# Moving one unit's scan by a slot or two, splitting three weight additions, and reordering loads in a scan-plus-MLP kernel

## The chip, the cores and the metric

The kernel runs on one core of one Trainium2 chip. The time is the device time of one execution in microseconds (us). The span that a profile covers is the part from the first to the last recorded instruction; the time is 1.7 us longer than its span. Before the change the median of the first three runs was 353.07 us (352.94 to 353.20).

## The reference

Two blocks follow each other. The first is a state-space scan (batch 4, 8 heads, 768 positions, head size 32, state size 16). The second multiplies its output, 3072 rows of 256, by a 256 x 2048 matrix, applies SiLU and multiplies by a 2048 x 256 matrix. All is in fp32.

```python
# first block, per chunk of the sequence (a clipped to [1e-6, 1])
L = exp(cum[i] - cum[j]) * (i >= j)            # decay between positions
y = ((C @ B.T) * L) @ x + (C @ state) * exp(cum)
state = decay_full * state + sum_j B_j x_j decay_from_j
# second block
h = x @ w_in
out = (h / (1 + exp(-h))) @ w_out
```

## The kernel before

The 3072 rows are cut into 12 units of 256 rows. Each unit goes through a scan: loads, transposes of its B and C (here `bn`, `tbc`), a decay matrix E by a VectorE scan over `ab`, B times decay (`BT`, on GpSimd), state products, and a product `y`, copied to `XM` by ScalarE. XM then feeds the first matrix product (`f_s1`, eight slots a unit, four matmuls each) and the second (`f_s2`). The scan's steps of later units are strewn between the slots of earlier ones, by hand, so that TensorE always has a matmul ready.

The loads of one unit stand on one queue in this order:

```python
def load_unit(u):
    load_pa(u, nc.sync)
    ...
    load_ab(u, nc.sync)        # clamped and scanned by VectorE
    load_n(u, 0, nc.sync)      # bn: transposed by TensorE
    load_x(u, nc.sync)
```

The weights come as raw pieces of 128 x 2 x 256 pairs of 32-bit words and are rebuilt on chip: two ScalarE activations (`w_size`), three VectorE operations, then one addition on GpSimd (`w_bits`, cut here):

```python
def w_bits(n, parts=1):
    ...
    for i in range(parts):
        fs = slice(WF // parts * i, WF // parts * (i + 1))
        nc.gpsimd.tensor_tensor(out=dst[:, :, fs]..., in0=u[:, :, fs], in1=v[:, :, fs], op=ALU.add)
```

A slot of the first product; `hp` comes from a pool of three PSUM buffers:

```python
def f_s1(g, j):
    hp = ps_h.tile([128, 2, UT], FP32, name="hp")
    for i in range(2):
        f = 2 * j + i
        for kc in range(KC):
            nc.tensor.matmul(out=hp[:, i], lhsT=w_in_sb[:, kc, f*128:(f+1)*128], rhs=xm[:, kc], ...)
    nc.scalar.activation(GTS[g][:, :, j], hp, AF.Silu)
```

The places of unit 2's steps (E = decay scan, D = BT, T and C = transposes and what follows, G = state products and masks, Y = y and XM; b and s = weight pieces), as (unit, slot, what follows the slot):

```python
steps = ((1, 0, "b5 s6"), (1, 1, "b6 s7"), (1, 2, "b7 s8"), (1, 3, "b8"), (0, 4, "E D"),
         (1, 4, ""), (0, 5, "T C s9"), (1, 5, "b9 s10"), (0, 6, "G"), (1, 6, "b10 s11"),
         (0, 7, "Y b11 s12"), (1, 7, "b12 s13"))
```

The loop over unit 3's slots, with unit 5's steps in between:

```python
for j in range(8):
    f_s1(3, j)
    ...
    scan_piece(5, j, ("", "", "T", "E", "DCS", "G", "YS", ""))
    ...
    f_s2(2 if j in (5, 6) else 4)
```

The very end of the kernel writes two last output tiles: each is transposed by TensorE, copied out of PSUM (one by ScalarE, one by VectorE) and stored, one from the SyncE queue and one from the ScalarE queue.

## Time and profile before

| | before |
|---|---|
| median of 3 runs | 353.07 us |
| the execution that was profiled | 355.06 us, span 353.3 us |
| TensorE busy | 343.8 us, 97% |
| TensorE weight loads | 287.5 us, 81% |
| VectorE, ScalarE, GpSimd busy | 58%, 46%, 32% |
| idle gaps of TensorE from 15 us to the last outputs | 3.05 us in six places |

The six gaps are read from the timeline of TensorE, where a bracket behind a group of instructions gives the idle time before it and what ended it. Those lines are in the prediction.

### The profile page before, as it was taken

To read this page: it belongs to the slowest core of one execution; us is meant where nothing else is said; L and a number is where in the kernel's file an instruction comes from. 1 tells how busy PE (TensorE), PEld (TensorE's weight loads), DVE (VectorE), ACT (ScalarE), POOL (GpSimd) and SP (SyncE) were. 2 spreads that over 40 slices of the span, in tenths; PEclk is the share of its full clock that TensorE was granted. 3 is DMA by queue.
4 is the path that set the end of the run, shared out by engine and by line. 5 is a ranking of instruction groups with operands and counts; after the bars stand their busy time and mean duration, and the time that the engine had idled before them with its cause. 6 is when DMAs were issued, how large, how long until landed. Compare 5 with 4: busy or idle time off the path is not lost.

```text
span 353.3 us, 8349 instructions
## 1 busy us (share of the span) xinstructions
PE 343.8 (97%) x3308; PEld 287.5 (81%) x3308; DVE 204.4 (58%) x408; ACT 162.0 (46%) x394; POOL 111.5 (32%) x137
## 2 busy tenths in 40 slices
PE   8979999999999999999999999999999999999995
PEld 3658778888888888888888888888888888888883
DVE  6997879978586663553664563564652232234821
ACT  2567487233323645454645445544545454453100
POOL 4344335554085041244041244041234112051200
PEclk9999999999999999999999999999999999999999
DMA  6986895699649398958179956057404237522202
GB/s 107 225 243 161 174 371 108 125 194 210 132 99 154 81 185 164 184 104 147 32 146 185 172 98 105 16 98 143 92 2 74 51 61 142 90 46 38 36 4 46
DMA packets 117376, 42.79 MB, mean 121 GB/s; under 512 B 102488, under 2 KB 109144, under 8 KB 117336
## 3 DMA queue, kind: packets, MB, share of 16 engines
q1 hardware_dynamic: 110328, 25.67, 34.7%
q0 software_dynamic: 4464, 16.25, 24.9%
q10 hardware_dynamic: 2544, 0.33, 0.6%
q8 instruction: 26, 0.43, 0.6%
q14 instruction: 14, 0.11, 0.1%
HBM read 22.83 MB, written 3.15 MB: 74 GB/s over the span
## 4 chain that ended last, share of the span: by engine, by line
PE 75%; DVE 9%; DMA 8%; SPq 5%; issue 2%; ACT 0%; ACTq 0%; DVEq 0%
PE o_ps L627 32%; PE hp L682 28%; PE hp L491 4%; PE hp L627 3%; DMA out_dram<-ot 2%; DMA ab<-in_a_dram 2%; SPq L95 2%; PE o_ps L613 2%; PE gy L467 2%; DVE E L303 1%; DVE E L415 1%; DMA raw<-in_moe_w_out_dram 1%; SPq L107 1%; PE gy L458 1%; DMA gT<-in_a_dram 1%
## 5 line engine op out<-in xcount | busy, mean ns | idle before, releaser
L685 DVE TENSOR_TENSOR gT<-hp,p 128x256 f32<-128x256 f32 x64 | 26.9, 420 | 73.8 <-ACT p L696 37.9
L491 PE MATMUL hp<-XM,w_in_sb 128*128 128x256 f32 x256 | 59.6, 382 | 2.0 <-POOL w_in_sb L182 2.0
L627 PE MATMUL o_ps<-gT,w_out_sb 128*128 128x256 f32 x240 | 60.4, 379 | 0.0
L688 ACT ACTIVATE gT<-gT 128x256 f32<-128x256 f32 x96 | 39.7, 414 | 44.0 <-DVE gT L685 43.9
L491 PEld LDWEIGHTS hp<-XM,w_in_sb 128*128 128x128 f32 x256 | 47.9, 190 | 10.0 <-POOL w_in_sb L182 3.3
L682 PE MATMUL hp<-raw 128*128 128x256 f32 x192 | 52.7, 380 | 0.0
L544 POOL TENSOR_TENSOR ps<-ps 128x256 f32<-128x256 f32 x35 | 29.2, 835 | 72.3 <-ACT ps L574 71.0
L627 PEld LDWEIGHTS o_ps<-gT,w_out_sb 128*128 128x128 f32 x240 | 45.4, 190 | 6.3
L539 POOL DMA_DIRECT2D gT<-gT x31 | 27.4, 921 | 64.9 <-PE hp L682 22.3
L682 PEld LDWEIGHTS hp<-raw 128*128 128x128 f32 x192 | 36.2, 190 | 5.4 <-POOL ps L544 0.6
L696 ACT ACTIVATE p<-hp 128x256 f32<-128x256 f32 x64 | 24.5, 383 | 27.5 <-PE hp L682 26.1
L685 DVE TENSOR_TENSOR gT<-hp,u 128x256 f32<-128x256 f32 x32 | 13.6, 425 | 39.3 <-PE hp L682 39.3
L682 PE MATMUL hp<-XM,w_in_sb 128*128 128x256 f32 x128 | 34.1, 389 | 0.0
L493 ACT ACTIVATE gT<-hp 128x512 f32<-128x512 f32 x32 | 19.0, 594 | 28.3 <-PE hp L491 28.2
L682 PEld LDWEIGHTS hp<-XM,w_in_sb 128*128 128x128 f32 x128 | 23.3, 190 | 4.3 <-issue 1.0
L303 DVE TENSOR_TENSOR_SCAN E<-ab,diag 128x256 f32<-128x256 f32 (+1 forms) x32 | 25.6, 842 | 0.4
L574 ACT ACTIVATE ps<-o_ps 128x256 f32<-128x256 f32 x38 | 14.4, 382 | 23.9 <-PE o_ps L627 22.2
L340 POOL TENSOR_TENSOR BT<-bn,E 128x256 f32<-128x256 f32 x12 | 9.0, 748 | 50.2 <-DVE E L303 48.9
L627 PE MATMUL o_ps<-gT,wu 128*128 128x256 f32 x88 | 22.4, 380 | 0.0
L627 PE MATMUL o_ps<-gT,wv 128*128 128x256 f32 x88 | 22.2, 380 | 0.0
L627 PE MATMUL o_ps<-gT,raw 128*128 128x256 f32 x80 | 20.6, 382 | 0.0
L682 PE MATMUL hp<-raw,w_in_sb 128*128 128x256 f32 x64 | 19.1, 380 | 0.0
(125 smaller groups left out, 518.7 us busy)
## 6 DMA issues: line engine op xcount, KB each, us to landing
gT<-gT POOLq DMA_DIRECT2D x31, 512.0 KB, 6.0
ab<-in_a_dram SPq DMA_DIRECT2D x40, 128.0 KB, 3.9
raw<-in_moe_w_in_dram SPq DMA_DIRECT2D x8, 512.0 KB, 6.3
raw<-in_moe_w_out_dram SPq DMA_DIRECT2D x8, 512.0 KB, 6.5
xt<-in_x_dram SPq DMA_DIRECT2D x24, 128.0 KB, 5.7
out_dram<-ot SPq DMA_DIRECT2D x92, 32.0 KB, 2.5
bn<-in_B_dram SPq DMA_DIRECT2D x22, 64.0 KB, 4.8
tbc<-in_C_dram SPq DMA_DIRECT2D x40, 32.0 KB, 1.8
```

The lines of the kernel that those rows point to most:

```text
L303: nc.vector.tensor_tensor_scan(out=E[u].rearrange("p k h t -> p (k h t)")[:, Q * g0:Q * (g0 + n)], data0=t.rearrange("p g t -> p (g t)"), ...
L340: engine.tensor_tensor(out=BT[u], in0=bn[u], in1=E[u][:, :, :, Q - 1:Q].to_broadcast([128, 2, H, N]), op=ALU.mult)
L491: nc.tensor.matmul(out=hp[:, i], lhsT=w_in_sb[:, kc, f * 128:(f + 1) * 128], rhs=xm[:, kc], start=(kc == 0), stop=(kc == KC - 1))
L493: nc.scalar.activation(GTS[g][:, :, j], hp, AF.Silu)
L539: nc.gpsimd.dma_start(out=o[:, js], in_=a[:, js], accum_op=ALU.add)
L544: engine.tensor_tensor(out=o, in0=p, in1=q, op=op)
L574: nc.scalar.activation(pn, on, AF.Copy)
L627: nc.tensor.matmul(out=o, lhsT=w(j), rhs=g()[:, j], start=(j == 0), stop=(j == last))
L682: nc.tensor.matmul(out=o, lhsT=w, rhs=x_, start=start, stop=True, skip_group_check=True)
L685: nc.vector.tensor_tensor(out=o, in0=p, in1=q, op=ALU.add)
L688: nc.scalar.activation(o, i, AF.Silu)
L696: nc.scalar.activation(o, i, AF.Copy)
```

## The change

The intent is to take away each of the six waits. Weight pieces 1 to 3 are added in halves, so that TensorE can begin on the first half. Unit 2's scan takes its transposes a slot earlier and its other steps one to two slots later. `bn` is loaded ahead of `ab`. Unit 2's y comes ahead of the first matmuls of the second product, and unit 5's y comes behind two of them.

```diff
 def load_unit(u):
+        load_n(u, 0, nc.sync)
         load_ab(u, nc.sync)
-        load_n(u, 0, nc.sync)
         load_x(u, nc.sync)
...
 def f_X(u):
-        nc.scalar.activation(XM[u], DP.pop(u)[:, :, 0:128], AF.Copy)
+        y = DP.pop(u)
+        n = 2 if u < 2 else 4
+        for i in range(0, 4, n):
+            nc.scalar.activation(XM[u][:, i:i + n], y[:, i:i + n, 0:128], AF.Copy)
...
-    w_bits(1)
+    w_bits(1, 2)            # and the same for pieces 2 and 3
...
-    steps = (..., (1, 3, "b8"), (0, 4, "E D"), (1, 4, ""), (0, 5, "T C s9"), (1, 5, "b9 s10"),
-             (0, 6, "G"), (1, 6, "b10 s11"), (0, 7, "Y b11 s12"), (1, 7, "b12 s13"))
+    steps = (..., (1, 3, "b8"), (0, 4, ""), (1, 4, "T"), (0, 5, "E D s9"), (1, 5, "C b9 s10"),
+             (0, 6, ""), (1, 6, "G b10 s11"), (0, 7, "b11 s12"), (1, 7, "Y b12 s13"))
...
 for j in range(8):           # unit 2's slots
+        f_s2(4 if j == 0 else 0)
         f_s1(2, j)
-        f_s2(2)
+        f_s2(2 if j > 0 else 0)
         ...
-        if j > 1:
-            f_s2(2)
+        f_s2(2 if j > 2 else 0)
...
 for j in range(8):           # unit 3's slots
         f_s1(3, j)
+        if j == 6:
+            f_s2(2)
         ...
-        f_s2(2 if j in (5, 6) else 4)
+        f_s2((4, 4, 4, 4, 4, 2, 0, 4)[j])
```

The rest of the diff makes a small helper tile (`mark`) five words smaller.

More of the change, by code (lines that the diff above doesn't have):

```diff
@@ L205 @@
     load_x(1, nc.sync)
-    mark = const.tile([1, RAW], U32, name="mark")
+    mark = const.tile([1, RAW - 5], U32, name="mark")
     for n in range(3, RAW):
         if n > 4:
-            nc.sync.dma_start(out=mark[:, n:n + 1], in_=raw[n - 2][0:1, 0, 0, 0:1])
+            nc.sync.dma_start(out=mark[:, n - 5:n - 4], in_=raw[n - 2][0:1, 0, 0, 0:1])
         load_w(n, nc.sync)
@@ L828 @@
     f_B(1)
-    w_bits(2)
+    w_bits(2, 2)
     f_C(1)
@@ L839 @@
     w_size(4)
-    w_bits(3)
+    w_bits(3, 2)
     w_bits(4)
@@ L845 @@
     f_s1(0, 3)
-    steps = ((1, 0, "b5 s6"), (1, 1, "b6 s7"), (1, 2, "b7 s8"), (1, 3, "b8"), (0, 4, "E D"),
-             (1, 4, ""), (0, 5, "T C s9"), (1, 5, "b9 s10"), (0, 6, "G"), (1, 6, "b10 s11"),
-             (0, 7, "Y b11 s12"), (1, 7, "b12 s13"))
+    steps = ((1, 0, "b5 s6"), (1, 1, "b6 s7"), (1, 2, "b7 s8"), (1, 3, "b8"), (0, 4, ""),
+             (1, 4, "T"), (0, 5, "E D s9"), (1, 5, "C b9 s10"), (0, 6, ""), (1, 6, "G b10 s11"),
+             (0, 7, "b11 s12"), (1, 7, "Y b12 s13"))
     def w_steps(todo):
```

## The prediction

> **What bounds the kernel now.** I read the page first, then the waits of TensorE, then the timeline of TensorE, then what each waited-for engine was doing at that time.
>
> ```profile
> PE 343.8 (97%) x3308; PEld 287.5 (81%) x3308; DVE 204.4 (58%) x408; ACT 162.0 (46%) x394; POOL 111.5 (32%) x137
> PE   8979999999999999999999999999999999999995
> ```
>
> TensorE is busy 97% of the span, and only the first three slices and the last fall short of nine tenths. A plain step of the products is one matmul, shown as two records; the timeline shows eight records (four matmuls) each 1.73 us, or 0.216 us a record. I call four such matmuls of the first product a slot. This change alters no matmul's shape or number, so it can win only idle time. All of it after 15 us stands in the timeline of TensorE, as the lines with a bracket:
>
> ```profile
> 18.14 1.99 PE L491 MATMUL hp<-XM,w_in_sb 128*128 128x256 f32 x8 [0.34 <-POOL w_in_sb L182]
> 22.07 1.99 PE L491 MATMUL hp<-XM,w_in_sb 128*128 128x256 f32 x8 [0.94 <-POOL w_in_sb L182]
> 26.21 14.08 PE L491 MATMUL hp<-XM,w_in_sb 128*128 128x256 f32 x64 [0.73 <-POOL w_in_sb L182]
> 40.59 0.75 PE L355 MATMUL o_ps<-ident,bn 128*128 128x128 f32 x2 [0.30 <-DMA bn<-in_B_dram]
> 50.15 0.69 PE L458 MATMUL gy<-cw,sm 32*64 32x64 f32 x32 [0.50 <-DVE E L415]
> 107.96 0.69 PE L458 MATMUL gy<-cw,sm 32*64 32x64 f32 x32 [0.24 <-DVE E L415]
> ```
>
> The columns are start, duration and instruction; the bracket is the idle time before it and who ended it. The sum is 0.34 + 0.94 + 0.73 + 0.30 + 0.50 + 0.24 = 3.05 us, 0.9% of the span. The transposes at 40.59 also take 0.75 us where the two just after them (tbc) take 0.38, because the second half of bn lands later: 0.37 us more, 3.42 in all. These six places are the targets: pieces 1 to 3 of the weights, the transposes of unit 2's bn, and the y of units 2 and 5. From 110 us to the end there is no wait, so what is won by then stays won and nothing more can be.
>
> **What the Trainium skill says.** "Perfetto Trace Analysis", section "Identifying the Most-Contended Engine", says that busy matmul time is no measure of nearness to the limit; so I took the gaps, and the equal 0.216 us steps between them, rather than the 97%. "GPSIMD Engine Reference", section "3.1 Elementwise", gives each GpSimd instruction a fixed dispatch cost, so halves should cost more in sum than a whole. The trace agrees: piece 0, already halved, takes 1.72 us, a whole piece 1.27. "SBUF — State Buffer", section "Who interferes with whom", has VectorE and GpSimd exclude each other from a shared pair of ports in some operations. The trace agrees: the shift on L176 takes 0.43 us alone and 1.37 beside a GpSimd addition (35.79). "DMA: Bandwidth & Descriptors", section "Queues, rings and completion order", has each DMA engine take a ring's descriptors in order; so what bn gains by going ahead of ab, ab loses. No run has shown this yet.
>
> **Part 1: pieces 1 to 3 in halves.**
>
> ```profile
> 14.46 1.72 POOL L182 TENSOR_TENSOR w_in_sb<-wu,wv 128x256 uint32<-128x256 uint32 x2 [3.06 <-DVE wv L178]
> 16.81 1.27 POOL L182 TENSOR_TENSOR w_in_sb<-wu,wv 128x512 uint32<-128x512 uint32 x1 [0.63 <-DVE wv L178]
> ...
> 20.76 1.26 POOL L182 TENSOR_TENSOR w_in_sb<-wu,wv 128x512 uint32<-128x512 uint32 x1 [0.96 <-DVE wv L178]
> 24.89 1.27 POOL L182 TENSOR_TENSOR w_in_sb<-wu,wv 128x512 uint32<-128x512 uint32 x1 [2.87 <-DVE wv L178]
> ```
>
> The slot's first two matmuls read only the first half, ready after 1.72 / 2 = 0.86 us instead of 1.27: 0.41 us sooner. The second half is ready 0.86 us later, just when two matmuls (0.86) are through. The three gains do not add up. Each addition starts when VectorE has finished its piece (the bracket), and VectorE is busy from 11.7 to 24.8 us without waiting for TensorE; so each gain only uses up the same lead, and what remains after piece 3 is 0.41. The longer additions fall beside scans and reads of PSUM, so I count no loss on VectorE. XM of units 0 and 1 in two halves costs ScalarE some 0.16 us each (0.38 x 2 less 0.60), off the path. Gain so far: 0.41.
>
> **Part 2: bn before ab, and the transposes one slot earlier.** The queue issues ab from 30.52 to 36.45 and bn to 37.74 us. In the new order bn is issued by about 35.5 and should land about 37.3. TensorE reaches the transposes at 40.13 - 1.73 - 0.41 = 37.99. The wait should vanish: 0.30 + 0.37 = 0.67. Gain at the state products of unit 2: 1.08.
>
> Ab lands up to a microsecond later. Unit 2's E waits for it (VectorE starts at 40.45) and GpSimd ends BT at 44.60. With the scan's products one slot later TensorE asks for BT at 44.94 + 1.73 - 1.08 = 45.59, so the delay fits.
>
> **Part 3: y of unit 2.** Here I expect part of the gain to be lost. The hp tile has three buffers, so the seventh slot of unit 0 needs the activation of the slot three before, which stands on ScalarE behind a weight piece that waits for its load:
>
> ```profile
> 45.79 0.67 ACT L164 ACTIVATE wu<-raw 128x512 f32<-128x512 f32 x1 [3.02 <-DMA raw<-in_moe_w_out_dram]
> 46.36 0.67 ACT L166 ACTIVATE wv<-raw 128x512 f32<-128x512 uint32 x1
> 46.94 0.57 ACT L493 ACTIVATE gT<-hp 128x512 f32<-128x512 f32 x1
> ```
>
> It ends at 47.51. Before, that slot started at 47.65, so the wait did not show. Now TensorE is there at 45.59 + 0.98 (the state products) = 46.57 and waits about 1 us if the load lands as before: the gain falls to 0.1. Then y no longer waits, because both slots stand ahead of it (47.55 + 3.46 = 51.0, against E ready at 50.0): + 0.50. Four matmuls of the second product (1.73) cover the copy to XM, which on ScalarE may end at 54.1, just in time. So 0.6 if the load of that weight piece is unmoved, up to 1.6 if it comes a microsecond sooner. That can be: the queue now stands still at xt until 39.98 with bn's many small packets outstanding, and these now go out earlier. I choose 0.9.
>
> **Part 4: unit 5.** Bn goes ahead of ab for every unit, and unit 5 is the one with no slack:
>
> ```profile
> 98.20 1.06 DVE L321 TENSOR_SCALAR ab<-ab 128x1024 f32<-128x1024 f32 x1 [0.81 <-DMA ab<-in_a_dram]
> 99.34 0.07 DVE L322 MEMSET ab<- 128x16 f32 x1
> 99.52 3.01 DVE L303 TENSOR_TENSOR_SCAN E<-ab,diag 128x512 f32<-128x512 f32 x2
> ```
>
> Its two bn issues take 1.2 us of the queue, so ab lands some 1.2 us later. Against that, the scan is slowed now (3.01, against 2.34 for unit 2) by four GpSimd additions from 96.75 to 101.44; started later it falls clear of them: -0.39 on L321 and -0.67 on the scan. E should be about where it was, BT too (it ends at 103.61), while TensorE asks for it 0.9 sooner, at 103.0; so up to 0.6 of the gain turns into a new wait there. I take 0.3. Putting two matmuls (0.86) before y covers the 0.24 wait and any such lateness of E. XM of unit 5 is not used before 114 us. Net: -0.3 + 0.24.
>
> **Sum.** 0.9 - 0.3 + 0.24 = 0.84; I add 0.3 because the loads follow VectorE, which also moves forward if the weight piece lands sooner. About 1.1 us: 353.07 - 1.1 = 351.9.
>
> **Rivals.** First, all waits vanish and nothing takes their place. The sum is then 0.41 + 0.67 + 0.50 + 0.24 = 1.8, with the unmovable part of the weight waits left: 351.2. For it: each part is aimed at one bracket. Against it: the activation at 47.51, which was not visible as a wait because it was met by 0.14 us. Second, ab's later landing becomes the bound in unit 5: if the scan is not quicker, BT is 1.2 us later (104.8), and TensorE starts there at 104.8 instead of 103.89. That eats everything: 353.07 - 0.24 + 0.9, with y then free, about 353.7. Against it: the GpSimd additions that now lie beside the scan. Third, the second product catches up with its weights (pieces 10 to 15 on GpSimd from 51.48 on, one each 2.36 us); before, the first use of piece 10 came 7 us after it was ready (60.30 against 52.87), so I give this little.
>
> **Range and chances.** 351.9 us, 351.0 to 352.9. The total idle time bounds the gain at 1%, and the worst rival loses less than 0.3%, so within 2% is nearly certain: faster 0.01, same 0.98, slower 0.01.
>
> **What would show it.** In the changed trace: the three weight brackets smaller by about 0.4 in total; no bracket on bn's transposes; a new bracket of up to 1 us on the first product near 46.6, ended by ScalarE; none on y of unit 2; a small one on unit 5's state products, ended by GpSimd's BT. If that last one is over 1 us, or the first product's bracket is missing, the working is wrong there.

## The result, and the profile after

| | before | after |
|---|---|---|
| median | 353.11 us (352.70 to 353.25, 6 runs) | 351.78 us (351.40 to 352.01, 6 runs) |
| ratio | | 0.9963, 95% interval 0.9951 to 0.9976 |

A ratio is the mean time of one kernel's runs over that of the other's in the same rounds, so it is not quite the ratio of the medians quoted. The change is worth 1.3 us, 0.4%, and within 2% it is "same". The predicted 351.9 was met almost to the decimal, but in good part by luck: most of the steps that led to it did not hold.

The page of the kernel after begins with its span and instructions, then gives the busy time of each engine and TensorE's busy tenths in 40 slices:

```profile
PE 343.5 (98%) x3307; PEld 287.6 (82%) x3308; DVE 205.7 (59%) x408; ACT 162.3 (46%) x396; POOL 112.4 (32%) x140
PE   8989999999999999999999999999999999999996
```

The busy time of TensorE is what it was, as it must be. ScalarE has two instructions more (the XM halves) and GpSimd three more (the weight halves).

The timeline of TensorE in the kernel after (start, duration, instruction, and in a bracket the idle time before it):

```profile
21.25 1.99 PE L495 MATMUL hp<-XM,w_in_sb 128*128 128x256 f32 x8 [0.56 <-POOL w_in_sb L182]
...
25.40 12.36 PE L495 MATMUL hp<-XM,w_in_sb 128*128 128x256 f32 x56 [0.38 <-POOL w_in_sb L182]
37.60 0.38 PE L355 MATMUL o_ps<-ident,bn 128*128 128x128 f32 x2
...
45.04 0.43 PE L389 MATMUL gy<-xt,BT 64*32 64x64 f32 x24
...
49.67 0.69 PE L458 MATMUL gy<-cw,sm 32*64 32x64 f32 x32
...
106.49 0.69 PE L458 MATMUL gy<-cw,sm 32*64 32x64 f32 x32
```

Between 15 us and the last outputs only two brackets are left, both on the weights (the transposes at the very end wait 0.38 us for VectorE in this kernel and 0.39 in the one before). The transposes of unit 2's bn (37.60) take 0.38 us and do not wait. The state products (45.04) and both y (49.67 and 106.49) do not wait either. At first sight that is the first rival of the prediction, in which every wait vanishes and nothing replaces it. But four vanished waits (0.30 + 0.37 + 0.50 + 0.24) and a gain on the weights would have made more than 1.3 us, unless the waits had not been there to begin with. That was my first question.

The GpSimd additions after (pieces 1 and 3), to be set against 1.27 us for a whole piece:

```profile
16.53 1.41 POOL L182 TENSOR_TENSOR w_in_sb<-wu,wv 128x256 uint32<-128x256 uint32 x2 [0.63 <-DVE wv L178]
...
24.61 1.61 POOL L182 TENSOR_TENSOR w_in_sb<-wu,wv 128x256 uint32<-128x256 uint32 x2 [2.72 <-DVE wv L178]
```

A pair of halves takes 1.41 us for pieces 1 and 2 and 1.61 for piece 3. Taken singly, the first half takes 0.72 to 0.74 us in all three, not the 0.86 that I had taken from piece 0.

ScalarE in the kernel after, at the place where I expected a new wait (the weight piece that stands ahead of the activation that frees an hp buffer):

```profile
42.14 0.67 ACT L164 ACTIVATE wu<-raw 128x512 f32<-128x512 f32 x1 [1.58 <-DMA raw<-in_moe_w_out_dram]
...
43.28 0.58 ACT L497 ACTIVATE gT<-hp 128x512 f32<-128x512 f32 x1
```

The activation ends at 43.86, against 47.51 in the profile before. The piece was there 3.7 us sooner, and the wait on hp did not form.

VectorE in the kernel after, unit 5's clamp of ab and its scan:

```profile
95.27 1.16 DVE L321 TENSOR_SCALAR ab<-ab 128x1024 f32<-128x1024 f32 x1
...
96.69 3.00 DVE L303 TENSOR_TENSOR_SCAN E<-ab,diag 128x512 f32<-128x512 f32 x2
```

Ab had landed in time even behind bn (no bracket), where the profile before showed 0.81 us of waiting for it. The scan is as long as before (3.00): GpSimd's four additions lie beside it here too (94.73 to 100.21 us).

### The profile page after: what moved, and what is told of

It reads as the page before. It is cut to its first block, busy times and chain, and to the rows that moved or that the text cites. A ratio compares the mean times of both kernels' runs of the same rounds, so it can differ in the third digit from the quotient of the medians.

```text
span 350.1 us, 8358 instructions
## 1 busy us (share of the span) xinstructions
PE 343.5 (98%) x3307; PEld 287.6 (82%) x3308; DVE 205.7 (59%) x408; ACT 162.3 (46%) x396; POOL 112.4 (32%) x140
## 3 DMA queue, kind: packets, MB, share of 16 engines
HBM read 22.83 MB, written 3.15 MB: 74 GB/s over the span
## 4 chain that ended last, share of the span: by engine, by line
PE 91%; DVE 4%; DMA 2%; issue 1%; SPq 0%; ACTq 0%; POOL 0%; ACT 0%; DVEq 0%
PE o_ps L631 36%; PE hp L686 28%; PE hp L495 15%; PE hp L631 3%; PE gy L467 2%; PE o_ps L617 2%; PE gy L404 2%; PE gy L458 2%; DMA gT<-in_a_dram 1%; PE gy L389 1%; DVE wv L178 1%; DVE E L415 1%; DMA tbc<-in_B_dram 1%; DVE st L430 0%; DMA out_dram<-ot 0%
## 5 line engine op out<-in xcount | busy, mean ns | idle before, releaser
L340 POOL TENSOR_TENSOR BT<-bn,E 128x256 f32<-128x256 f32 x12 | 9.4, 782 | 47.8 <-DVE E L303 39.6
```

Of the source, the lines that this page charges most:

```text
L340: engine.tensor_tensor(out=BT[u], in0=bn[u], in1=E[u][:, :, :, Q - 1:Q].to_broadcast([128, 2, H, N]), op=ALU.mult)
```

## The experiments

Twelve runs were made, in three groups, each group on one chip (numbers 6, 14 and 9) with its own runs of the kernel before. All their outputs were correct and all their executions count as fast; four of them (356.3 to 357.4 us, in runs 3, 7 and 8) had a mean granted clock of 0.995 and are much longer than the others of their kernel, so I quote medians and ranges beside the ratios. Times of the kernel before in the three groups: medians 353.05, 353.11 and 353.07 us, with single executions up to 353.94, 353.71 and 355.26.

To compare traces whose starts differ by a few tenths, I count TensorE from its first y product (unit 0, near 13 us) to the first matmul of the last phase that reads a weight from `raw` (`hp<-raw`, near 112 us), called the start of the last phase below. From there to the end of TensorE all traces take 234.6 to 234.9 us. The third quantity is the tail, from the end of TensorE's last record to the end of the span.

### 1. The kernel before, once more

The edit: none.

> The kernel before, unchanged, as a control. Its first profile was of an execution of 355.06 us, 2 us over its own median of 353.07. Theory A (that profile was of an unusually late execution): a new profile has a span near 351.4 and brackets on TensorE after 15 us that sum to 1 to 2 us instead of 3.05. Rival B (the profile was typical and the 2 us are the profiler's): span near 353.3 again and brackets near 3. Ratio of times 1.000 within 0.001 in both.

Measured: 353.13 us (353.04 to 353.57, 4 runs), ratio 1.0004 (0.9991 to 1.0017). The execution profiled took 353.04 us, span 351.3. Its timeline of TensorE:

```profile
17.94 1.99 PE L491 MATMUL hp<-XM,w_in_sb 128*128 128x256 f32 x8 [0.33 <-POOL w_in_sb L182]
...
21.88 1.99 PE L491 MATMUL hp<-XM,w_in_sb 128*128 128x256 f32 x8 [0.94 <-POOL w_in_sb L182]
...
26.03 14.08 PE L491 MATMUL hp<-XM,w_in_sb 128*128 128x256 f32 x64 [0.74 <-POOL w_in_sb L182]
39.95 0.38 PE L355 MATMUL o_ps<-ident,bn 128*128 128x128 f32 x2
...
48.57 0.69 PE L458 MATMUL gy<-cw,sm 32*64 32x64 f32 x32
...
106.07 0.69 PE L458 MATMUL gy<-cw,sm 32*64 32x64 f32 x32
```

The three waits on the weights are the same to 0.01 us. The other three are gone, in the very same kernel: the transposes at 39.95 take 0.38 us without a bracket, and neither y waits. So 0.30 + 0.37 + 0.50 + 0.24 = 1.41 us of the waits that I set out to win belonged to one slow execution. In that one the last part of unit 2's bn landed at 40.97 us, while 15 of the 16 DMA engines had finished theirs by 39.95; of ab, 40.32 against 39.53. The raw piece that held up ScalarE landed at 45.70, and at 41.04 in the run here.

Two things come together there. The queue was late: it issued bn at 36.50 and 37.16 us, and at 33.70 and 34.37 in the run here, where 15 parts of the second bn load had landed by 37.10. Why the queue was late is not known. And a 16th part came late on top. That is not peculiar to the slow execution (unit 2's ab has one here, 0.55 to 0.76 us behind the other 15), but there it met bn. The view of the DMA queues of the slow execution from 37.9 to 41 us has, next to the loads, one packet of 16 KiB on queue 8, which is marked "instruction" (it runs from 37.97 to 38.85), and behind the loads a thin train of 7 to 12 GB/s (39.6 to 40.6 us):

```profile
GB/s 326 81 87 67 100 134 143 138 134 122 101 90 110 121 121 104 98 52 33 28 21 17 7 12 9 9 9 9 9 8 9 9 9 9 9 30 73 92 121 114
...
q8 instruction: 1, 0.02, 1.8%
```

Over the loads of ab, bn, tbc, x and raw pieces that SyncE issued after 50 us in all fourteen traces (those whose 16 parts landed within 9 us), the 16th part comes 0.43 us (median) after the 15th where a queue 8 packet was under way between issue and landing (813 loads), and 0.06 us where none was (1110). So a fetch of instructions is the likely cause of the late part; the traces do not say which engine carried the packet, so it is not shown. The prediction's 0.81 us of waiting for unit 5's ab was of that execution too: here that clamp starts at 95.72 us without a wait, and the scan behind it takes 3.01.

### 2. Only the halves

```diff
-    w_bits(1)          # and 2, 3
+    w_bits(1, 2)
-        nc.scalar.activation(XM[u], DP.pop(u)[:, :, 0:128], AF.Copy)
+        (XM in two halves for units 0 and 1, as in the change)
```

> Only the additions of pieces 1 to 3 (and the copies of units 0 and 1) in halves. Prediction: 0.41 us, ratio 0.9988. Rival 1 (the three gains add up): 1.2 us, ratio 0.9966. Rival 2 (the gain is eaten by the later wait on bn or on y of unit 2, which stand at times that follow the loads): 0, ratio 1.000.

Measured: 352.78 us (351.90 to 354.76, 6 runs), ratio 0.9997 (0.9976 to 1.0019). The interval is too wide to tell 0.5 us from nothing. The trace tells more: unit 0's fourth slot (piece 3) starts 12.54 us after the first y, against 13.08 in both traces of the kernel before. That is 0.54 us, and the last phase starts 99.28 us after the first y against 99.82, again 0.54. The tail is 3.92 us, as before (3.86 and 3.90).

### 3. Only bn ahead of ab

```diff
 def load_unit(u):
+        load_n(u, 0, nc.sync)
         load_ab(u, nc.sync)
-        load_n(u, 0, nc.sync)
```

> Only bn ahead of ab in the queue, for all units; nothing moves on TensorE. My working: the bracket on the transposes of unit 2 (0.67 with its tail) goes, but unit 2's BT is late for the state products, which stand one slot earlier here (asked for at 44.3, ready at 45.2 or so), and y of unit 2 still waits: gain 0 to 0.5, ratio 0.9986 to 1.000. Rival (the load of the weight piece comes sooner because small packets no longer hold up the queue): E of unit 2 and its y sooner by up to 1 us, ratio about 0.997.

Measured: 353.42 us (352.10 to 356.34, 6 runs), ratio 1.0016 (0.9984 to 1.0048). The timeline of TensorE at the state products of unit 2:

```profile
45.14 0.43 PE L389 MATMUL gy<-xt,BT 64*32 64x64 f32 x24 [1.20 <-POOL BT L340]
```

Here is a price of the order, where the scan's place is not moved as well: ab comes later, BT is late, and TensorE waits 1.20 us. The size belongs to this execution: the last load of ab had 15 parts by 39.21 us and the 16th at 40.53, where the kernel after, with the same order, has all by 38.14. The last phase starts at 101.08, 1.26 us later than in run 1. But the tail is 3.29 us, 0.6 shorter than before. Nothing in the order of unit 2's loads should touch the last four microseconds of the kernel, and this was not in my prediction at all.

### 4. Only the scan's places

```diff
-    steps = (... (0, 4, "E D"), (1, 4, ""), (0, 5, "T C s9"), ...)
+    steps = (... (0, 4, ""), (1, 4, "T"), (0, 5, "E D s9"), ...)
...
+        f_s2(4 if j == 0 else 0)
         f_s1(2, j)
-        f_s2(2)
+        f_s2(2 if j > 0 else 0)
-        if j > 1:
-            f_s2(2)
+        f_s2(2 if j > 2 else 0)
```

> Only unit 2's scan moved (transposes one slot sooner, state products one slot later, y two slots... after both slots, then four matmuls of the second product); ab still ahead of bn. My working: the transposes now wait about 2 us for bn (reached at 38.4, bn there at 40.6), the state products and y wait for nothing: slower or equal, ratio 1.000 to 1.003. Rival (in usual executions bn is early): faster by 0.5 us or more, ratio 0.9985.

Measured: 353.39 us (352.84 to 354.21, 6 runs), ratio 1.0010 (0.9996 to 1.0024). By itself this part wins nothing, which follows from run 1: the waits that it removes are not there in a usual execution. Its last phase starts at 100.06 (0.24 later than in run 1, with transposes of 0.57 us, since they now ask for bn a slot sooner), and its tail is 3.60. The wait of some 2 us on bn that I expected did not come: bn had landed by 38.31 us, not 40.6.

### Looking at the tail

The tail of the kernel before (run 1), from the timeline: VectorE's copy of the last output tile and the issue of its store.

```profile
347.90 0.29 DVE L600 COPY ot<-hp 128x128 f32<-128x128 f32 x1 [0.92 <-PE hp L595]
348.22 0.37 ACTq L603 DMA_DIRECT2D out_dram<-ot  x1
```

And of the kernel after:

```profile
347.25 0.29 DVE L604 COPY ot<-hp 128x128 f32<-128x128 f32 x1 [0.73 <-DMA out_dram<-ot]
347.58 0.37 ACTq L607 DMA_DIRECT2D out_dram<-ot  x1
```

From the last issue to the end of the span it is 351.3 - 348.2 = 3.1 us before and 350.1 - 347.6 = 2.5 us after, for the same 64 KB. The view of the DMA queues says what is in the way. For the last 3.9 us of run 1, GB/s in 40 equal slices, then queues with packets, MB and share of 16 engines:

```profile
GB/s 0 0 0 0 0 0 0 0 0 21 215 273 200 5 0 0 0 95 268 231 69 11 5 11 16 11 0 0 0 0 0 0 0 0 0 0 0 0 0 0
...
q14 instruction: 1, 0.01, 1.1%
```

For the last 3.3 us of the kernel after:

```profile
GB/s 0 0 0 0 0 0 0 0 0 0 0 0 0 93 298 267 131 6 0 0 155 323 236 81 0 0 0 0 0 0 0 0 0 0 0 0 0 0 0 0
...
q10 hardware_dynamic: 144, 0.07, 6.8%
```

There are two humps in each, the two last stores. In the kernel before, the second hump has a thin train behind it (11, 5, 11, 16, 11 GB/s). Queue 14 sent one packet then, of 8192 bytes, which took 0.67 us; in the kernel after, queue 14 is absent from the end. Queue 14 is marked "instruction": a block of instructions is fetched while the last outputs leave. That fits one late engine out of 16: of the second-last store 15 engines' parts land 2.27 to 2.44 us before the end and the 16th 1.08; of the last store 15 land 1.52 to 1.66 before the end and the 16th 0.90. In the kernel after, all 16 of the second-last store land between 1.47 and 1.65 before the end and all of the last between 0.91 and 1.09. The Trainium skill, "CRC Debugging", section "Comparing the Two Runs", calls queue 14 that of the sequencers' instruction refills; the trace agrees.

Why does the change move a fetch? The page "Runtime: NRT & Kernel Launch", section "Instruction fetch mechanics", gives 256 instructions for 16 KiB, so an estimate of 128 for these 8192 bytes. VectorE's instruction number at four of the fetches is about 191, 318, 446 and 575, which is that spacing. With bn ahead of ab, four of VectorE's clamps of ab wait for two loads where they waited for none before, and each such wait is one instruction more: at the line of the clamps the trace has 32 records instead of 28, and VectorE, counted with its waits, has 584 instead of 580. Four instructions more ahead of the boundary bring the fetch forward, out of the last stores. That VectorE is the engine whose block it is, is inferred from the spacing; the trace does not name it (runs 5 and 10 add to this).

This could be tried without any of the change, by adding four instructions that do nothing.

### 5. The kernel before with four empty instructions

```diff
+    pad = const.tile([1, 4], FP32, name="pad")
...
 for j in range(8):           # unit 3's slots
+        if j == 1:
+            for i in range(4):
+                nc.vector.memset(pad[:, i % 4:i % 4 + 1], 0.0)
```

> The kernel before plus four empty memsets of one element each on VectorE near 90 us, where it idles for 5 us; nothing of the change is in it. The trace of the changed kernel has four more instructions on VectorE than the one of before (584 against 580), all waits that follow from the new order of loads, and its last instruction fetch (an 8192-byte packet) falls before the last products and not into the output's last packets. Theory T (the fetch in the tail costs 0.8 us: one DMA engine lands the last output late and VectorE's last copy starts late): the fetch moves forward, the time from the end of TensorE to the end of the span falls from 3.9 to 3.1 us, ratio 0.9977. Rival (the shorter tail is chance or belongs to the order of loads): ratio 1.000, tail 3.9.

Measured: 352.33 us (351.97 to 352.71, 5 runs) against 353.11 (352.65 to 353.71, 11 runs), ratio 0.9980 (0.9967 to 0.9992). Four memsets of one element each make the kernel 0.8 us quicker. TensorE's way to the last phase is 99.82 us, exactly that of run 1, so the gain is all in the tail: 2.95 us. The DMA queues of its last 3.1 us:

```profile
GB/s 0 0 0 0 0 0 0 0 0 0 0 0 0 0 152 277 271 132 13 112 297 278 139 20 0 0 0 0 0 0 0 0 0 0 0 0 0 0 0 0
...
q1 hardware_dynamic: 144, 0.07, 7.3%
```

Two clean humps and no queue 14. The last fetch comes 5.25 us before the end instead of 2.74.

### 6. The halves with the four empty instructions

The edit: that of run 2 and that of run 5 together.

```diff
-    w_bits(1)          # and 2, 3
+    w_bits(1, 2)
+    (XM of units 0 and 1 in halves; four memsets on VectorE)
```

> The halves of pieces 1 to 3 plus the four empty memsets; neither the order of loads, nor unit 2's scan, nor unit 5's y. Theory T and halves together are the whole gain: 0.45 on TensorE plus 0.8 in the tail, ratio 0.9965, as the full change (0.9963). Rival (the other parts of the change are worth something in a usual execution): ratio 0.998 or above, slower than the full change.

Measured: 352.27 us (352.06 to 352.77, 5 runs), ratio 0.9978 (0.9966 to 0.9990). That is no more than run 5 alone; the 0.54 us of the halves does not show. The fourth slot does start at 12.53, and then the gain goes: TensorE comes to unit 2's transposes sooner than bn does (they take 0.62 us instead of 0.38; of bn's last load 15 parts landed by 38.42 and the 16th at 39.68), and unit 5's y waits:

```profile
106.40 0.69 PE L459 MATMUL gy<-cw,sm 32*64 32x64 f32 x32 [0.45 <-DVE E L416]
```

The last phase starts at 100.14, later than without the halves. So in this execution the halves needed the other parts to keep what they won.

### 7. All but the order of loads

```diff
 (from the kernel after)
-        load_n(u, 0, nc.sync)
         load_ab(u, nc.sync)
+        load_n(u, 0, nc.sync)
```

> The full change with ab ahead of bn again. Theory T: VectorE is back at 580 instructions or near, the fetch is back in the tail, and 0.8 us are lost: ratio to before 0.9987. Rival (the order of loads helps by landing bn early): TensorE waits for bn at unit 2's transposes, a bracket there of 0.3 us or more; and the tail stays at 3.1.

Measured: 354.31 us (352.42 to 357.44, 6 runs), ratio 1.0044 (1.0004 to 1.0084). The profiled execution was one of the four long ones (356.67 us), so its wait is read as a kind and not as a size:

```profile
40.15 0.72 PE L355 MATMUL o_ps<-ident,bn 128*128 128x128 f32 x2 [2.28 <-DMA bn<-in_B_dram]
```

With the transposes a slot earlier and bn still behind ab, TensorE runs into bn. VectorE is back to 580 instructions, the fetch is back in the tail (2.43 us before the end), and the tail is 3.57. Even its two quickest executions, 352.42 and 352.64, are above all six of the kernel after in the result above.

### 8. All but the halves

```diff
 (from the kernel after)
-    w_bits(1, 2)       # and 2, 3
+    w_bits(1)
-    (XM of units 0 and 1 in halves)
+    (XM whole)
```

> The full change with pieces 1 to 3 (and the copies of units 0 and 1) whole again. Prediction and theory T: 0.45 us of the gain is lost, ratio to before 0.9976, three brackets near 0.33, 0.94, 0.74 as before and the tail at 3.1. Rival (the halves only use up a lead that other waits give back): ratio 0.9963, as the full change.

Measured: 352.57 us (352.26 to 356.40, 6 runs), ratio 1.0004 (0.9973 to 1.0035), with one execution at 356.40 that widens the interval. By the medians it is 0.8 us above the kernel after (351.78). In the trace the fourth slot is back at 13.07, and TensorE waits for BT:

```profile
46.45 0.43 PE L389 MATMUL gy<-xt,BT 64*32 64x64 f32 x24 [0.46 <-POOL BT L340]
```

The tail keeps its gain (3.30 us, fetch 5.94 before the end).

### 9. The whole change, once more

The edit: none against the kernel after.

> The full change unchanged, as a control on whatever chip the next three run on. Ratio 0.9963 within 0.001; brackets on TensorE only at the weights; tail from the end of TensorE to the end of the span 3.1 us.

Measured: 351.88 us (351.49 to 354.04, 6 runs) against 353.07 (352.55 to 355.26, 11 runs), ratio 0.9969 (0.9941 to 0.9997). Fourth slot 12.54, last phase 99.37, tail 3.16: the first result holds in a second set of rounds.

### 10. The whole change with 124 more empty instructions

If the place of the fetch is what counts, a nearly full block of instructions more should bring the next fetch to where the old one was, and undo the gain.

```diff
 (from the kernel after, in the loop over the last phase)
+            if (G, j) != (2, 0):
+                for i in range(4):
+                    nc.vector.memset(pad[:, i:i + 1], 0.0)
```

> The full change plus 124 empty memsets of one element on VectorE, four after each of 31 steps of the later products, where VectorE is idle most of the time. Theory T: instructions are fetched in blocks of 8192 bytes, 128 of them, and with 584 + 124 = 708 the last fetch stands as far from the end as with 580: it is back in the tail, the tail is 3.9 again, and 0.7 to 0.8 us of the gain are gone: ratio 0.9985. TensorE's own timeline as in the full change, its end within 0.2 us. Rival (the tail is short for another reason in the new order): tail 3.1, ratio 0.9963, or slower only by what the memsets cost TensorE, which its brackets would show.

Measured: 352.00 us (351.65 to 352.98, 6 runs), ratio 0.9968 (0.9943 to 0.9993). This expectation failed. VectorE counted 704 instructions and not 708, because its four waits for a second load were gone again (169 waits against 173), so the next fetch did not come into the last stores but 0.64 us after the end of the span. The tail is 2.94. The trial therefore did not show the reversal that it was made for. It is one more trace with no fetch in the last stores and a short tail. It does show whose fetch it is: with nothing added but VectorE's memsets, the fetch that stands at 344.36 us in the kernel after, at about VectorE's 575th instruction, stands at 269.31 us, at about its 576th.

### 11. Halves, unit 5's y and the four empty instructions

```diff
 (run 6, and)
+        if j == 6:
+            f_s2(2)
-        f_s2(2 if j in (5, 6) else 4)
+        f_s2((4, 4, 4, 4, 4, 2, 0, 4)[j])
```

> Halves, unit 5's y behind two products, and four empty memsets; order of loads and unit 2's scan as before. In the halves with pads alone unit 5's y waited 0.45 us, which ate the halves. Theory: with its y later nothing waits, TensorE ends 0.5 us sooner than in the kernel before, tail 3.1: ratio 0.9963, as the full change, so unit 2's parts are worth nothing in a usual execution. Rival (unit 2's parts carry something): 0.998.

Measured: 352.35 us (351.40 to 353.02, 6 runs), ratio 0.9971 (0.9947 to 0.9994). Unit 5's y no longer waits, but the transposes of bn take 0.67 us, and the last phase starts at 99.79. Some executions are as quick as the kernel after (351.40) and others are not.

### 12. All but unit 5's y

```diff
 (from the kernel after)
-        if j == 6:
-            f_s2(2)
-        f_s2((4, 4, 4, 4, 4, 2, 0, 4)[j])
+        f_s2(2 if j in (5, 6) else 4)
```

> The full change with unit 5's y in its old place. Theory: as in the halves with pads, TensorE is at unit 5's y before E is, and a bracket of 0.2 to 0.5 us by VectorE is back: ratio 0.9973 or so, tail 3.1. Rival (the new order of loads moves E as well): no bracket, 0.9963.

Measured: 351.89 us (351.63 to 352.24, 6 runs), ratio 0.9962 (0.9940 to 0.9983). I expected a small bracket on unit 5's y, and there was none. This part is worth nothing in a usual execution of the full change. It is also the nearest to a version that beats the kernel after, and it only ties with it.

### The traces side by side

| kernel | VectorE instr. | last fetch before the end, us | last issue to the end, us | tail, us | fourth slot, us | last phase, us |
|---|---|---|---|---|---|---|
| before (slow execution) | 580 | 2.72 | 3.05 | 3.86 | 13.08 | 101.53 |
| before, run 1 | 580 | 2.74 | 3.10 | 3.90 | 13.08 | 99.82 |
| only halves | 580 | 2.43 | 3.11 | 3.92 | 12.54 | 99.28 |
| only scan | 580 | 2.43 | 2.80 | 3.60 | 13.08 | 100.06 |
| all but the load order | 580 | 2.43 | 2.76 | 3.57 | 12.58 | 103.79 |
| before + 4 empty | 584 | 5.25 | 2.50 | 2.95 | 13.09 | 99.82 |
| only bn ahead of ab | 584 | 5.91 | 2.48 | 3.29 | 13.08 | 101.08 |
| halves + 4 empty | 584 | 5.86 | 2.49 | 3.22 | 12.53 | 100.14 |
| all but the halves | 584 | 5.94 | 2.47 | 3.30 | 13.07 | 100.34 |
| all but unit 5's y | 584 | 5.74 | 2.48 | 3.15 | 12.55 | 99.29 |
| after | 584 | 5.71 | 2.49 | 3.10 | 12.54 | 99.47 |
| after, run 9 | 584 | 5.76 | 2.47 | 3.16 | 12.54 | 99.37 |

Runs 10 and 11 fit in (2.49 and 2.48 us from the last issue to the end). The fetch falls in the last stores in five traces, and there the last issue is 2.76 to 3.11 us from the end; in the other nine it is 2.47 to 2.50. There is no exception. The rest of the tail, from TensorE's end to the copy, does not part the two groups cleanly: 0.47 to 0.49 us in the five, 0.12 to 0.51 in the nine.

But a part of it does. In the five traces that last copy is VectorE's 576th instruction and starts 0.40 to 0.41 us after the end of the wait before it; in the nine it is the 580th (the 700th in run 10) and starts 0.04 us after. The same delay stands at 448 and 192, which are 128 and 3 x 128 before 576: ahead of VectorE's 448th instruction in runs 5, 6 and 11 (0.40 us; the same instruction is the 444th in the five, 0.04 there), and ahead of unit 5's clamp of ab where it is the 192nd (0.41 to 0.49 us in eleven traces; 0.05 in runs 5, 6 and 11, where the four empty instructions make it the 196th). Ahead of the 320th, which follows not a wait but another operation, no delay shows. So the boundary costs twice in the last stores: some 0.36 us ahead of the copy, and 0.3 to 0.6 us in the landing of the stores. In run 5 the two are 0.35 + 0.60 = 0.95 us, all of the difference in the tail (3.90 to 2.95).

## Why the prediction was right or wrong

The time was right: 351.9 was said, and 351.78 and 351.88 were measured. Its steps make that luck: of the predicted 1.1 us on TensorE only 0.35 to 0.45 us is there (99.82 less 99.47 and less 99.37), and the other part of the gain is the tail, of which it said nothing: 3.90 - 3.10 = 0.80 and 3.90 - 3.16 = 0.74 us. Together 1.15 and 1.19, against 1.33 and 1.19 between medians.

**What bounds the kernel now.** The reading that TensorE is the bound and that only its gaps can be won was right up to TensorE's last matmul. The step that failed is "These six places are the targets". Three of the six, with the stretched transposes 1.41 of 3.42 us, belonged to the profiled execution and not to the kernel (run 1). The sign was on the page: 355.06 us against a median of 353.07. The statement that nothing more can be won after 110 us was wrong too, since the last stores were not looked at. And the gaps were read in one execution (355.06) but subtracted from the median of others (353.07).

**Part 1, the halves.** Mechanism right, one term mis-sized. Piece 3's first half took 0.74 us and not 1.72 / 2 = 0.86; piece 0's pair, from which I took it, runs slower than the other three. 1.27 - 0.74 = 0.53, against 0.54 measured and 0.41 said. That the three gains would not add up held: 0.54 once. The brackets fell by more than 0.4, from 0.33 + 0.94 + 0.74 = 2.01 to 0.56 + 0.38 = 0.94, but a bracket counts only idle time ahead of a group. In the profiled execution of the kernel after, unit 1's second part of y took 1.12 us instead of 0.86, and the moment when the fourth slot starts is the better measure.

**Part 2, bn ahead of ab.** The wait went, as said, but 0.67 us was not there to be won. The warning that ab would be later and that the scan's later place would hide it fits the runs: in its trace the order alone costs 1.20 us at BT (run 3), the later place alone wins nothing (run 4), and together TensorE reaches BT at 45.04 without a wait. The sizes are those of single executions.

**Part 3, y of unit 2 and the hp buffer.** Wrong on both sides. The 0.50 of y was of the slow execution, and so was the late weight piece behind which the hp buffer was to be freed: the activation ended at 43.86 us instead of 47.51 (and in run 1, the kernel before, at 43.38). The new bracket near 46.6 us, which the prediction named as the sign that its working holds, is missing. (The slot in question is the one numbered 7, so the eighth of unit 0 and not the seventh.) The two errors nearly cancelled (0.50 won against 1 us lost).

**Part 4, unit 5.** The 0.3 loss did not come. Ab was in time, BT without a bracket. The scan did not get quicker (3.00 us where I counted on 0.67 less), because it did not fall clear of GpSimd's four additions, and it did not need to. The 0.24 won at y was of the slow execution, and run 12 shows that the two matmuls ahead of y are worth nothing here.

**The sum.** 0.9 - 0.3 + 0.24 + 0.3 stood for 0.41 + 0.67 + 0.50 + 0.24 less new waits. What there was: 0.54 from the halves, of which 0.35 to 0.45 had been kept at the last phase (in the trace of the kernel after, 0.18 us goes at unit 3's y, where products that take 0.86 us in run 2 take 1.04; why, I did not settle), and 0.75 to 0.8 in the tail: 0.61 from the last issue to the end (3.10 to 2.49), and 0.47 - 0.29 = 0.18 from the earlier copy. (The copy's delay at the boundary fell by 0.35, but in the kernel after the copy also waits for an earlier store, as its bracket shows.)

**The rivals.** In the first, all waits vanish: right as to the waits, wrong as to the time, because most of them were not there. The second, ab's lateness in unit 5, did not appear; its like in unit 2 did, where the scan had been left in place. The third, the weights of the second product, had no sign in any trace.

**The parts depend on each other.** The halves bring TensorE to bn sooner, so they need bn earlier (run 6). Bn earlier makes ab later, so it needs the scan later (run 3). The scan's earlier transposes need bn earlier (run 7). The load order also brings the four extra waits that move the fetch, so run 7 loses both. The waits behind these three are read from one trace each, and the place of the loads varies between executions: the queue issues the first of unit 2's ab and bn at 27.5 to 30.6 us in the fourteen traces, latest in the slow execution of the kernel before (30.5) and in runs 7 (30.6) and 8 (30.4). Run 2, with the halves alone, had no wait on bn. So the directions are likely, and the sizes open.

**What stays open.** That the place of VectorE's instructions relative to the fetch makes the tail long is shown by run 5 as cause (four empty instructions, 0.78 us between medians) and by the table without exception; the trial in the other direction (run 10) missed its mark. That the block is VectorE's the trace does not say in words, but the spacing, run 10 and the delays at its 192nd, 448th and 576th instructions, which move with the four empty ones, leave little doubt. Four empty instructions could in principle act through something else that they move, but TensorE takes the same 99.82 us to the last phase in runs 1 and 5. Why some executions of several kernels are 1 to 5 us longer is not settled; in the one that I looked at, the queue issued unit 2's loads 2.8 us later than in run 1, and one part out of 16 came later still.

## What to carry to other kernels

Before you read waits from a profile, hold the time of the profiled execution against the median; where they differ by as much as you hope to win, profile the same kernel again. A change that adds or takes away a few waits or instructions also moves the points at which instructions are fetched, and in the last stores that can be worth as much as the change itself: four empty instructions are a cheap control. Measure a sub-microsecond gain at a point in the trace that all variants pass, and not by the sum of the brackets.

## What the Trainium skill lacked or had wrong

- "Runtime: NRT & Kernel Launch", section "Instruction fetch mechanics", calls the cost of a block boundary "mostly hidden". In the last stores of this kernel it was not: 2.76 to 3.11 us from the last issue to the end with a fetch there, 2.47 to 2.50 without; 0.40 us between a wait and the instruction at the boundary, 0.04 elsewhere; and 0.78 us between medians in run 5.
- The same section gives 16 KiB blocks. Here queue 14 moved 14 packets of 8192 bytes, four of them some 128 VectorE instructions apart; queue 8, also marked as instruction, moved 26 packets of 16 KiB.
- "DMA: Bandwidth & Descriptors", section "Queues, rings and completion order", has the refill among the queues that share the 16 DMA engines, but no page that I read says what a fetch costs a store: with one, the 16th part of the second-last store landed 1.08 us before the end, the other 15 at 2.27 to 2.44 (run 1).
- "GPSIMD Engine Reference", section "3.1 Elementwise", has the fixed cost of an instruction but not what two halves cost: 1.41 us against 1.27 for the whole, and 1.60 to 1.72 for other pairs of the same size in the same kernel.
- No page that I read gives a size for one late part of a load out of 16, or says that it varies between executions ("DMA: Bandwidth & Descriptors", section "Latency and other measured facts", calls two of the engines usually slower): unit 2's bn landed at 40.97 us on one engine and by 39.95 on the other 15 in one execution, at 37.41 and 37.10 in the next.
